# Order of a unit's high and low matmuls in the sequence stage of a fused FNet and GEGLU layer

## Chip, cores and metric

The kernel runs on one core of a Trainium2 chip. The metric is device time in microseconds of one execution of the whole program; lower is better. Times are medians of several runs.

## The reference

One token sequence of S = 2048 rows and D = 448 columns is normalised, goes through a Fourier mixing layer and through a gated feed-forward layer of width 1792, and the two results are multiplied and added to the input.

```python
xn = layernorm(x)                                   # (1, 2048, 448)
a = einsum("bsd,ed->bse", xn, dft_hid_re)
b = einsum("bsd,ed->bse", xn, dft_hid_im)
s = einsum("ts,bse->bte", dft_seq_re, a) - einsum("ts,bse->bte", dft_seq_im, b)
g = silu((gelu(xn @ w_gate) * (xn @ w_up)) @ w_down)
out = x + s * g
```

All inputs and the output are float32.

## The kernel before

**Numbers in two halves.** Matmuls read a float32 format that keeps fewer bits (`float32r`). To keep accuracy, an operand is split into a high half (the rounded value, made by ScalarE) and a low half (value minus high half, made by VectorE), and a product is summed from several matmuls: high by high, high by low, low by high.

**Stages.** Rows are in 16 blocks of 128. First come layer norm, transposes and the feed-forward layer with its Strassen-like schemes (`strassen`, `three`, `down_one`); then the transform along the hidden dimension (`hid_mm`, line 1105); then the last stage, the transform along the sequence, which this case is about. It starts at about 477 us of the span. The program is written in the order in which each engine issues it (`manual_schedule`), so the order of the calls in the code is the order on TensorE, ScalarE, VectorE, GpSimd and of the DMA queue of SyncE (SP).

**Last stage.** The output rows come in 8 groups, `j`, of two row blocks each. For each group the 16 blocks of input rows, `k`, are gone through. Fourteen of them (`KS`) are done with a scheme of Strassen's kind, in which the 2 by 2 product of (two output blocks) by (real and imaginary part) times (two halves of the columns) takes seven products. The other two (`KP`) are done plainly, as units `t0` and `t1`, line 1309 to 1311, 12 matmuls of 448 columns each. So a group has `UN` = 16 units, `m` counts the units of all groups, and `u` = `m % UN` is the place in the group; `NS` = 14.

A Strassen unit has 14 matmuls (`seven`). For each of the seven products `q` in the order of `PRODUCTS` (1, 6, 2, 7, 5, 3, 4) there is

- a *high* matmul (line 1289): high half of the coefficient block `i` as weights, 128 by 128, and the 448 columns `v` of the data tile `TS[k]`, block `b`, which holds high half and low half of 224 values beside each other;
- a *low* matmul (line 1292): low half of the same coefficient block, and the first 224 columns of `v` alone.

Each product has its own PSUM bank and is accumulated there over the fourteen units. The eighth bank takes `t0`; `t1` takes the bank that product 1 has left. For the next group the banks are rotated by one (`banks[1:] + banks[:1]`), so that its product 1 gets the bank in which product 6 was, and so on; the seventh gets that of `t0`.

**Around it.** The coefficient blocks of unit `m` are loaded from HBM by SP (`load_c`, lines 1181 to 1188), two of them are summed by VectorE (`sum_c`, lines 1194 and 1195), and `prep_c` splits them: ScalarE writes the high halves (line 149), VectorE the low ones (line 150), into one of four slots. In unit `m` the program issues, in this order: the matmuls; for `u` from 0 to 7, one DMA (line 1365) that overwrites a part of a data tile for the next group; `sum_c(m + 4)`; then what the unit's place asks for, in most `prep_c(m + 3)`, with `load_c(m + 8)` behind it.

**End of a group.** In the last Strassen unit (`u` = 13), `gather` combines the seven products: ScalarE copies product 1 from its bank (line 1317), and VectorE then goes through the others in the order 6, 2, 7, 5, 3, 4 (lines 1319 to 1325). Three of these operations are issued at `u` = 13, the rest behind `sum_c` at `u` = 14. The multiplication by the gate, the addition of the input and the stores follow in small steps during the next group.

**End of the kernel.** In the last group the last three Strassen units (`LAST` = 3) are not done one behind another. Their 21 steps (product, unit) are put in an order (`last_steps`) in which products 1, 6 and 2 are finished early and the others one by one:

```python
last_steps = [(q, n) for n, k in ((0, 4), (1, 3), (2, 3)) for q in order_[:k]]
last_steps += [(q, n) for q in order_[3:] for n in range(LAST) if (q, n) not in last_steps]
```

so steps 1 to 10 are products 1, 6, 2, 7 of the first unit, 1, 6, 2 of the second, 1, 6, 2 of the third. Step 8 finishes product 1. Behind them TensorE does `t0` and `t1`, while VectorE does `gather` and the final arithmetic (lines 1383 to 1402); the last stores are issued at line 1403.

Of the kernel before, what the change touches and what calls it, by code (L numbers as in the profile page):

```python
# [13 lines left out]
P = 128  # L14
S = 2048
D = 448
# [11 lines left out]
HD = D // 2  # L28
# [18 lines left out]
NS = len(KS)  # L47
# [4 lines left out]
def order(j):  # L52

    return [*KX[j % 2], *KR, *KX[(j + 1) % 2]]
# [5 lines left out]
def fnet_geglu(ctx: ExitStack, tc: tile.TileContext, xw, ca, ct, cp, et, wss, wd, out):  # L60
# [15 lines left out]
    nc = tc.nc  # L76
# [51 lines left out]
    def bank(i, name):  # L128
        return psum.tile([P, 512], F32, name=name, tag=f"b{i}")
# [421 lines left out]
    with tc.manual_schedule():  # L551
# [356 lines left out]
        h, l = [[v[:, n] for n in range(4)] for v in (xth[1], xtl[1])]  # L908
# [61 lines left out]
        for n, (p, f) in enumerate(blocks):  # L970
            g = f // 2
            dn, q = [send] * 4, tq[p]
# [8 lines left out]
            if p == 0:  # L981
# [12 lines left out]
                if f in (8, 11):  # L994

                    k = slice(0, 4, 3) if f == 8 else slice(1, 3)
                    for i in range(2):
                        v, w = [u[:, i * 2048 :][:, :2048] for u in (sp, a_x[1].bitcast(F32))]
                        v, w = [u.rearrange("p (k d) -> p k d", k=4)[:, k] for u in (v, w)]
                        nc.sync.dma_start(v, w)  # L1000
            elif f == 2:
                q = None
# [3 lines left out]
            elif f == 3:  # L1006

                late = then(late[0], t1_steps[7][2]), late[1]
                v = sb.tile([P, 8 * D], F32, name="gacc2", tag="u1")
# [3 lines left out]
                v = sb.tile([P, 4096], FR, name="w2", tag="u0")  # L1013
# [76 lines left out]
        TS, ab, behind = {}, {}, []  # L1090
# [4 lines left out]
        def hid_mm(k):  # L1095
            c, kk = divmod(k, 4)
            sl = slice(kk * P, (kk + 1) * P)
            ps = []
            for r in range(2):
                p = in_turn("x" if k < 2 else "all", f"ab{k}_{r}")  # L1100
                mm = [(xth[c][:, b, sl], e_at[b][r]) for b in range(4)]
                mm += [(xth[c][:, b, sl], e_at[b][2 + r]) for b in range(3)]
                mm += [(xtl[c][:, b, sl], e_at[b][r]) for b in range(4)]
                for n, (a, b) in enumerate(mm):
                    nc.tensor.matmul(p[:, :D], a, b, start=n == 0, stop=n == len(mm) - 1)  # L1105
                ps.append(p[:, :D])
            return ps
# [44 lines left out]
        units = [(j, k) for j in range(NK // 2) for k in order(j) + ["t0", "t1"]]  # L1152
        UN = NS + 2
# [43 lines left out]
        c_hl = {}  # L1197
# [15 lines left out]
        for k in [*range(14), 15, 14]:  # L1213
            ps = hid_mm(k)
# [54 lines left out]
                nc.sync.dma_start(gx[t], gv[:, 2 * j + t])  # L1269


        LOAD_AT = 2
        STORE_AT = 6, 9
        GX_AT, GX_END = (NS, 0), (11, 12)
# [2 lines left out]
        PRODUCTS = {1: (1, 0), 6: (3, 5), 2: (2, 2), 7: (5, 3), 5: (4, 4), 3: (6, 6), 4: (0, 1)}  # L1277
# [3 lines left out]

        def seven(m, ps, steps=None):

            for q, n in steps or [(q, 0) for q in PRODUCTS]:
                i, b = PRODUCTS[q]
                u = m + n
                v = TS[units[u][1]][:, b * D : (b + 1) * D]
                h, l = [w[:, i * P : (i + 1) * P] for w in c_hl[u]]
                nc.tensor.matmul(  # L1289
                    ps[q][:, :D], h, v, start=u % UN == 0, stop=False, skip_group_check=True  # L1290
                )
                nc.tensor.matmul(  # L1292
                    ps[q][:, :HD], l, v[:, :HD],
                    start=False, stop=u % UN == NS - 1, skip_group_check=True,
                )


        order_ = [*PRODUCTS]
# [45 lines left out]
        for m, (j, k) in enumerate(units):  # L1344
            u = m % UN
            end = j == NK // 2 - 1
            if u == 0:
                ps = {q: bank(banks[i], f"p{q}_{j}") for i, q in enumerate(PRODUCTS)}
            if k in KS:
                if not end or u < NS - LAST:  # L1350
                    seven(m, ps)
                elif u == NS - LAST:

                    seven(m, ps, last_steps)

                at = (0, 1, 2, 3, 4, 5, 6, 7) if j else range(LOAD_AT, LOAD_AT + 8)
                for i in range(8):
                    if u != at[i]:
                        continue
                    i, h = divmod(i, 4)  # L1360
                    TS[KX[(j + 1) % 2][i]] = TS[KX[j % 2][i]]
                    n = KX[(j + 1) % 2][i]
                    a, b = [v.rearrange("p (b d) -> p b d", d=D) for v in (TS[n], td[n])]
                    a, b = a[:, PARTS[h]], b[:, PARTS[h]]
                    nc.sync.dma_start(a.bitcast(F32), b)
            else:
                py = bank(banks[7 if k == "t0" else 0], f"py{k[1]}_{j}")
                plain(m, py)
# [131 lines left out]
```

## Time and profile before

| | us |
|---|---|
| median of 3 runs | 768.38 |
| lowest and highest | 768.17, 768.41 |
| profiled execution | 768.08 |
| its span in the profile | 766.3 |
| TensorE matmuls busy | 760.0 |
| weight loads busy (overlap with matmuls) | 685.6 |
| VectorE busy | 641.7 |
| ScalarE busy | 351.4 |

The profile is of one execution. PE is TensorE, PEld its weight loads, DVE is VectorE, ACT is ScalarE, POOL is GpSimd, SP is SyncE, whose queue issues most DMAs; SPq and ACTq are DMA issues of these engines. A row of the timeline has the start in us, the duration in us, the engine, the line of the kernel, the operation, the tiles that it writes and reads (out<-in), the shape, how many instructions are merged in the row, and in brackets how long the engine was idle before it and what ended this. A row of a group has busy us, mean ns of one, and idle time. Weight loads have a row of their own before the matmul that uses them. The recorded duration of a matmul is modelled and reaches beyond the start of the next one; the distance between two starts is the better measure of its cost. A matmul of float32r has a weight load of its own each time.

### The profile page before, as it was taken

How to read it: one execution, taken by the hardware profiler on the slowest of the kernel's cores; microseconds unless marked ns; L12 is line 12 of the kernel's file. 1: busy time of each engine (PE TensorE's matmuls, PEld its weight loads, DVE VectorE, ACT ScalarE, POOL GpSimd, SP SyncE). 2: the span in 40 equal slices, each digit the busy share in tenths (PEclk: the TensorE clock that was granted, in tenths of full speed). 3: DMA queues.
4: the chain of work that ended last, by engine and by line, in shares of the span. 5: the costliest groups of instructions: out<-in, count | busy, mean ns of one | idle time of the engine just before them, and what ended most of it. 6: DMA issues, size and time to landing. Idle time of an engine off the chain costs nothing.

```text
span 766.3 us, 11490 instructions
## 1 busy us (share of the span) xinstructions
PE 760.0 (99%) x4041; PEld 685.6 (89%) x4041; DVE 641.7 (84%) x1087; ACT 351.4 (46%) x499; POOL 122.8 (16%) x162
## 2 busy tenths in 40 slices
PE   9999999999999999999999999999999999999997
PEld 8988888888888888888889999999999999999997
DVE  7987789999989888988876677988889797979786
ACT  5866433444435334343344755544444344444441
POOL 2002332422434224232200000000000000000000
PEclk9999999999999999999999999999999999999999
DMA  8077484949568563738642732869696969788794
GB/s 299 15 223 233 118 246 138 233 154 243 205 142 298 139 207 82 223 79 245 153 184 85 296 165 69 279 224 338 209 352 206 341 213 311 248 279 277 246 324 153
DMA packets 81034, 162.28 MB, mean 212 GB/s; under 512 B 8016, under 2 KB 62800, under 8 KB 79568
## 3 DMA queue, kind: packets, MB, share of 16 engines
q1 hardware_dynamic: 75648, 135.02, 51.5%
q0 software_dynamic: 5184, 26.41, 16.1%
q8 instruction: 32, 0.52, 0.3%
q14 instruction: 26, 0.21, 0.1%
q10 hardware_dynamic: 144, 0.11, 0.0%
HBM read 139.36 MB, written 51.25 MB: 249 GB/s over the span
## 4 chain that ended last, share of the span: by engine, by line
PE 98%; DVE 1%; issue 0%; ACT 0%; DVEq 0%
PE x L444 24%; PE p L1289 21%; PE po L422 18%; PE p L1292 10%; PE ab L1105 9%; PE x L456 4%; PE gu L371 3%; PE gu L592 2%; PE py L1309 1%; PE py L1311 1%; PE py L1310 1%; PE pt L206 1%; PE warm L571 1%; PE pt L649 0%; DVE cc L1384 0%
## 5 line engine op out<-in xcount | busy, mean ns | idle before, releaser
L422 PE MATMUL po<-wd,hs 128*128 128x448 f32 x672 | 152.7, 366 | 0.0
L422 PEld LDWEIGHTS po<-wd,hs 128*128 128x128 f32 x672 | 125.8, 188 | 14.2
L444 PE MATMUL x<-xt,w 128*128 128x512 f32 x432 | 114.1, 391 | 0.0
L444 PEld LDWEIGHTS x<-xt,w 128*128 128x128 f32 x432 | 81.1, 188 | 15.3
L149 ACT ACTIVATE w<-raw 128x896 fp32r<-128x896 f32 (+1 forms) x59 | 53.6, 910 | 61.9 <-DVE raw L1195 22.4
L444 PE MATMUL x<-t,w 128*128 128x512 f32 x276 | 80.8, 391 | 0.0
L433 DVE TENSOR_TENSOR gacc<-gacc,po 128x448 f32<-128x448 f32 x96 | 58.5, 615 | 14.3 <-PE po L422 14.2
L1105 PE MATMUL ab<-w,xt 128*128 128x448 f32 x256 | 68.1, 365 | 0.0
L521 ACT ACTIVATE hs<-tmp 128x512 fp32r<-128x512 f32 x24 | 15.2, 633 | 101.1 <-DVE tmp L519 101.1
L444 PEld LDWEIGHTS x<-t,w 128*128 128x128 f32 x276 | 51.8, 188 | 9.3
L1289 PE MATMUL p<-xt,w 128*128 128x448 f32 x168 | 54.3, 374 | 0.0
L320 POOL TENSOR_TENSOR raw<-raw 128x256 f32<-128x256 f32 x23 | 19.7, 858 | 212.0 <-DMA raw<-wss 158.2
L1334 POOL DMA_DIRECT2D cc<-xw x14 | 12.3, 881 | 252.8 <-DVE raw L1194 96.1
L1105 PEld LDWEIGHTS ab<-w,xt 128*128 128x128 f32 x256 | 48.1, 188 | 3.8
L149 ACT ACTIVATE w<-f 128x896 fp32r<-128x896 f32 (+1 forms) x34 | 30.2, 888 | 41.7 <-DVE f L1195 17.4
L150 DVE TENSOR_TENSOR w<-raw,w 128x896 fp32r<-128x896 f32 (+1 forms) x40 | 41.8, 1046 | 2.0 <-ACT w L149 1.4
L339 ACT ACTIVATE w<-raw 128x768 fp32r<-128x768 f32 x24 | 20.3, 846 | 39.8 <-POOL raw L326 39.8
L1289 PE MATMUL p<-ts_g,w 128*128 128x448 f32 x112 | 36.3, 374 | 0.0
L1289 PE MATMUL p<-ts_u,ts_tmp 128*128 128x448 f32 x112 | 36.3, 374 | 0.0
L1289 PE MATMUL p<-hs,w 128*128 128x448 f32 x112 | 35.5, 374 | 0.0
L1105 PE MATMUL ab<-wd,xt 128*128 128x448 f32 x96 | 35.1, 365 | 0.0
L1289 PEld LDWEIGHTS p<-xt,w 128*128 128x128 f32 x168 | 31.5, 188 | 2.4
(297 smaller groups left out, 1849.6 us busy)
## 6 DMA issues: line engine op xcount, KB each, us to landing
sums<-ca SPq DMA_DIRECT2D x16, 896.0 KB, 8.8
sums<-ca POOLq DMA_DIRECT2D x16, 896.0 KB, 9.8
raw<-ct SPq DMA_DIRECT2D x69, 192.0 KB, 4.2
raw<-wss SPq DMA_DIRECT2D x24, 512.0 KB, 3.8
ts_u<-td SPq DMA_DIRECT2D x24, 448.0 KB, 5.7
ts_g<-td SPq DMA_DIRECT2D x24, 448.0 KB, 6.5
raw<-sums SPq DMA_DIRECT2D x69, 128.0 KB, 4.1
f<-ct SPq DMA_DIRECT2D x39, 192.0 KB, 4.5
```

Source lines behind the costliest of these rows:

```text
L149: nc.scalar.activation(h, src, AF.Copy)
L150: nc.vector.tensor_sub(l, src, h)
L320: eng.tensor_add(r[:, 1:16:14], r[:, 0:14:13], r[:, 9:17:7])
L339: nc.scalar.activation(h[:, :n], src[:, :n], AF.Copy)
L371: nc.tensor.matmul(ps[:, cols], a, xt[:, k, cols], start=n == 0, stop=n == len(mm) - 1)
L422: nc.tensor.matmul(po[:, :D], hs[:, a, kk * P : (kk + 1) * P], wdn[:, b, i], start=n == 0, stop=n == 5,)
L433: nc.vector.tensor_add(ga, ga, po[:, :D])
L444: nc.tensor.matmul(ps, a[i], b[j], start=first and n == 0, stop=n == 2, skip_group_check=True)
L456: nc.tensor.matmul(ps, a[0], x_, start=False, stop=True, skip_group_check=True)
L1105: nc.tensor.matmul(p[:, :D], a, b, start=n == 0, stop=n == len(mm) - 1)
L1289: nc.tensor.matmul(ps[q][:, :D], h, v, start=u % UN == 0, stop=False, skip_group_check=True)
L1292: nc.tensor.matmul(ps[q][:, :HD], l, v[:, :HD], start=False, stop=u % UN == NS - 1, skip_group_check=True,)
```

## The change

`seven` no longer issues high and low of each product in turn. It takes the steps in runs of `TOGETHER` = 7 and issues the high matmuls of a run first, then the low ones in the same order. A plain unit is one run; the 21 steps of the last three units are three runs: products 1, 6, 2, 7 of the first and 1, 6, 2 of the second unit; 1, 6, 2 of the third, 7 of the second and third, 5 of the first and second; and the rest of 5, 3 and 4. The flag that starts an accumulation stands on the high matmul of the group's first unit, the one that ends it on the low matmul of its last. Operands, counts, banks and everything on the other engines are as before.

```diff
+        TOGETHER = 7
...
         def seven(m, ps, steps=None):
 
-            for q, n in steps or [(q, 0) for q in PRODUCTS]:
-                i, b = PRODUCTS[q]
-                u = m + n
-                v = TS[units[u][1]][:, b * D : (b + 1) * D]
-                h, l = [w[:, i * P : (i + 1) * P] for w in c_hl[u]]
-                nc.tensor.matmul(
-                    ps[q][:, :D], h, v, start=u % UN == 0, stop=False, skip_group_check=True
-                )
-                nc.tensor.matmul(
-                    ps[q][:, :HD], l, v[:, :HD],
-                    start=False, stop=u % UN == NS - 1, skip_group_check=True,
-                )
+            steps = steps or [(q, 0) for q in PRODUCTS]
+            for at in range(0, len(steps), TOGETHER):
+                for part in range(2):
+                    for q, n in steps[at : at + TOGETHER]:
+                        i, b = PRODUCTS[q]
+                        u = m + n
+                        v = TS[units[u][1]][:, b * D : (b + 1) * D]
+                        w = c_hl[u][part][:, i * P : (i + 1) * P]
+                        d = D if part == 0 else HD
+                        nc.tensor.matmul(
+                            ps[q][:, :d], w, v[:, :d],
+                            start=part == 0 and u % UN == 0,
+                            stop=part == 1 and u % UN == NS - 1,
+                            skip_group_check=True,
+                        )
```

## The prediction

> **What bounds the kernel now.** I read the page first (busy times, then the chain that ended last), then single instructions of the last stage in the timeline.
>
> ```profile
> PE 760.0 (99%) x4041; PEld 685.6 (89%) x4041; DVE 641.7 (84%) x1087; ACT 351.4 (46%) x499; POOL 122.8 (16%) x162
> PE 98%; DVE 1%; issue 0%; ACT 0%; DVEq 0%
> L1289 PE MATMUL p<-xt,w 128*128 128x448 f32 x168 | 54.3, 374 | 0.0
> 546.00:580.00 34.00, 34.00 (x214) 32.36 (x213) 28.53 (x55) 15.47 (x18) 1.76 (x2) 1.00 0.89 287
> ```
>
> The page, the chain, a group of the high matmuls, and a stretch inside the last stage (columns: PE, PEld, DVE, ACT, POOL busy, granted clock, DMA share). TensorE carries 98% of the chain and has no idle time before the high matmuls; the clock is granted in full. VectorE, at 28.53 of 34 us, is behind it but not far. So the change is worth what it does to TensorE's pace, plus what it does where TensorE is not the last: the end.
>
> The pace first. These are the first high matmul of group 1, the first matmul behind its fourteen units, and from the chain a long run of matmuls of 448 columns, each with other weights than the one before.
>
> ```profile
> 512.65 0.36 PE L1289 MATMUL p<-ts_u,ts_tmp 128*128 128x448 f32 x1
> ...
> 543.35 0.38 PE L1309 MATMUL py<-ts_u,w 128*128 128x448 f32 x1
> 419.20 57.96 PE ab L1105 x286
> ```
>
> Fourteen units are 98 pairs of a high and a low: 30.70 / 98 = 0.3133 us a pair. A 448-column matmul behind another takes 57.96 / 286 = 0.2027 us. So a low (224 columns) costs 0.3133 - 0.2027 = **0.1106 us**, and everything turns on what it costs behind another low.
>
> **The change part by part.** No matmul, weight load, DMA or elementwise instruction is added or removed; only the order on TensorE differs, in 112 runs of seven products (8 groups of 14 units, the last three units of the last group being shared out over three such runs). In each run 7 lows stand in a row, so 6 x 112 = 672 lows are followed by a low instead of a high; six of seven highs are followed by a high. The trace of before has no low behind a low, and I bound it by neighbours.
>
> ```profile
> 561.28 0.19 PEld L1289 LDWEIGHTS p<-xt,w 128*128 128x128 f32 x1
> 561.38 0.38 PE L1289 MATMUL p<-xt,w 128*128 128x448 f32 x1
> 561.38 0.19 PEld L1292 LDWEIGHTS p<-xt,w 128*128 128x128 f32 x1
> 561.59 0.27 PE L1292 MATMUL p<-xt,w 128*128 128x224 f32 x1
> 561.59 0.19 PEld L1289 LDWEIGHTS p<-xt,w 128*128 128x128 f32 x1
> 561.69 0.37 PE L1289 MATMUL p<-xt,w 128*128 128x448 f32 x1
> 561.70 0.19 PEld L1292 LDWEIGHTS p<-xt,w 128*128 128x128 f32 x1
> ```
>
> Beside them, transposes and matmuls of 256 columns from the first stage (the same run of matmuls seen in two windows, one of which ends a matmul later).
>
> ```profile
> 45.78 0.60 PE L206 MATMUL pt<-ident,xr 128*128 128x128 f32 x4
> 46.11 0.30 PEld L422 LDWEIGHTS po<-wd,hs 128*128 128x128 f32 x2
> L206 PE MATMUL pt<-ident,xr 128*128 128x128 f32 x32 | 4.8, 272 | 0.0
> 13.78 0.88 PE L592 MATMUL gu<-xt,w 128*128 128x256 f32 x6
> 13.78 1.00 PE L592 MATMUL gu<-xt,w 128*128 128x256 f32 x7
> ```
>
> Each weight load starts when the matmul before its own starts, never earlier (561.28 beside the low before it, 561.38 with the high at 561.38, 561.59 with the low at 561.59): one load ahead and no more. Behind a low, the next load follows 0.10 to 0.11 us later (561.28 to 561.38, 561.59 to 561.70): the load of the next high's weights just fills the low's time. The transposes have only 128 columns to stream, and yet four of them, 0.272 us long each, span 0.60 us: (0.60 - 0.272) / 3 = 0.109 us apart, with the next load at 46.11 right behind the fourth's start. That is the pace of weight loads alone. Matmuls of 256 columns take 1.00 - 0.88 = 0.12 us each. A line through 448 and 256 columns (0.2027 and 0.120) puts the streaming of 224 columns at 0.106 us.
>
> So a low behind a low lies between 0.106 (streaming alone) and 0.120 (a matmul of 256 columns cannot be quicker than one of 224). I take the larger of loads and streaming, **0.109**: the 224-column low is nearest the transposes, which loads bound. It was bound by a load before, too, since a high's load ran under it; grouping does not change how many loads run under lows, seven per unit either way. That gains 672 x (0.1106 - 0.109) = **1.1 us**; at the bounds, 3.1 us gained or 6.3 us lost. The highs behind highs cost their 0.2027 in both orders. The first low of a unit, whose load waits for VectorE's low half, comes 1.42 us into the unit (7 x 0.2027) instead of 0.20, and the high half's wait on ScalarE keeps its place.
>
> Next, the ends of the groups. A product is complete with its low in the last unit. The first product, which ScalarE copies out and the whole combining in `gather` waits for, was complete 0.31 us into the unit and now is at 7 x 0.2027 + 0.11 = 1.53 us: **1.21 us later**. At the end of group 1:
>
> ```profile
> 541.16 0.37 PE L1289 MATMUL p<-ts_g,w 128*128 128x448 f32 x1
> 541.67 0.55 ACT L1317 ACTIVATE cc<-p 128x448 f32<-128x448 f32 x1 [1.93 <-PE p L1292]
> 542.24 0.62 DVE L1319 TENSOR_TENSOR cc<-cc,p 128x448 f32<-128x448 f32 x1 [0.81 <-ACT cc L1317]
> ...
> 547.16 0.62 DVE L1325 TENSOR_TENSOR cc<-p,cc 128x448 f32<-128x448 f32 x1
> ...
> 548.22 0.36 PE L1289 MATMUL p<-ts_u,ts_tmp 128*128 128x448 f32 x1
> ```
>
> ScalarE's copy moves from 541.67 to 542.9, and VectorE, which already waits for it (0.81 us idle), moves all its later work by 1.2 us: the last bank is read by 547.16 + 0.62 + 1.2 = 548.98. The next group starts at 548.22 and now takes all its banks within seven highs; the one just freed is the sixth's, at 548.22 + 5 x 0.2027 = 549.23. Spare: 0.25 us. Tight, but I cost it at nothing; if the spare were gone, every microsecond would be paid at seven group ends. Behind the late reads on VectorE stand the weight halves of the units ahead and, behind those, SP's loads of their raw blocks. The closest of these low halves that I found:
>
> ```profile
> 714.36 1.08 DVE L150 TENSOR_TENSOR xt<-raw,ts_tmp 128x896 fp32r<-128x896 f32 x1
> 716.83 0.38 PE L1289 MATMUL p<-ts_u,ts_tmp 128*128 128x448 f32 x1
> ```
>
> It is done at 715.44 and was wanted by the first low at 717.03; now that low comes at 716.83 + 1.42 = 718.25, so 1.2 us of delay leaves the old distance. SP's reloads of the tiles for the next group wait for a product of units 0 to 7 that finishes up to 1 us later, but have until unit 12. No cost.
>
> Last, the end of the kernel, where nothing covers that delay.
>
> ```profile
> 750.21 0.38 PE L1289 MATMUL p<-xt,w 128*128 128x448 f32 x1
> 752.61 0.27 PE L1292 MATMUL p<-ts_g,w 128*128 128x224 f32 x1
> 752.91 0.55 ACT L1317 ACTIVATE cc<-p 128x448 f32<-128x448 f32 x1 [0.80 <-PE p L1292]
> 753.50 0.62 DVE L1319 TENSOR_TENSOR cc<-cc,p 128x448 f32<-128x448 f32 x1 [0.66 <-ACT cc L1317]
> ...
> 755.48 0.62 DVE L1322 TENSOR_TENSOR cc<-cc,p 128x448 f32<-128x448 f32 x1
> ...
> 761.46 0.37 PE L1311 MATMUL py<-xt,ts_tmp 128*128 128x448 f32 x1
> 761.86 0.62 DVE L1400 TENSOR_TENSOR f<-ts_g,py 128x448 f32<-128x448 f32 x1
> 762.52 0.69 DVE L1402 TENSOR_TENSOR cc<-cc,f 128x224 f32<-128x224 f32 x2
> 753.50:763.20 9.70, 8.32 (x47) 7.47 (x45) 9.32 (x17) 0.00 (x0) 0.00 (x0) 1.00 0.13 42
> ```
>
> The last three units start at 750.21; the closing low of product 1, their eighth step, starts 2.40 us later at 752.61, ScalarE copies, and from 753.50 VectorE is busy 9.32 of 9.70 us to the end: a dense chain. L1400 starts just as the last matmul is done (761.46 + 0.37 = 761.83) and as VectorE itself is free. In the new order the steps go in three runs of seven, and step 8 is the first of the second run: its low stands behind one run (7 x 0.3133 = 2.19) and seven highs (1.42), 3.61 us in. The chain starts 3.61 - 2.40 = **1.2 us later**; the other products are complete before their turn (the fifth, product 5, closes with the first low of the third run, at 750.21 + 2 x 2.19 + 1.42 + 0.27 = 756.3, and is wanted at 755.48 + 1.2 = 756.7), so VectorE carries all of it to the last store.
>
> Sum, against the profiled execution's own 768.08 us (span 766.3 and 1.8 around it): 768.08 - 1.1 + 1.2 = 768.2. That execution lies 0.3 below the median of the three runs, 768.38, so on their scale **768.5 us**: no change, two small terms against each other.
>
> **The rivals.** *Lows in a row are dearer* (slower): a load may start only once the low before has really started, and streaming and loading may not overlap as fully as under a high. A line between 128 and 256 columns (0.109 and 0.120) gives 0.117 for 224: 672 x 0.008 = 5.4 us above my sum, 773.9. It decides early: with 1.2 us lost at the end, 0.111 a low is already over 0.2%. For it: both limits lie within 3 ns of each other, and nothing in the trace shows them together. Against: 256 columns hide a load at 0.120 with nothing visible on top.
>
> *Group ends run dry* (slower): if VectorE's reads come 0.5 us later than I count, TensorE waits 0.25 us seven times, 1.8 us: 770.3. For: the spare is small. Against: the reads move rigidly with ScalarE's copy.
>
> *Loads get ahead* (faster): if the lows' weights were loaded while highs stream, a low would take the 0.101 us that stands between its start and the next high's. 672 x 0.0096 = 6.5 us, with the end's loss 763.1 on the runs' scale. The rows above, one load ahead each time, speak against it. The Trainium skill speaks for it, page "TensorE: Matmul & The Clock Gate", section "Back-to-back issue gap": loads are pulled ahead through a 64-deep window and 128-column matmuls are sustained at about 81 ns, 512-column ones at 131. By a line through these, an estimate from that page, a low would take 93 ns and the sum be about 757; the trace's 0.11 us for 128 columns and 0.2027 for 448 disagree with both figures, so I go by the trace.
>
> That the change does not do what it says I leave out: the order on TensorE is the order of the program.
>
> **How the numbers follow.** No change, 0.48, with its own range of 767.4 to 769.9 (0.107 to 0.111 a low). Lows dearer, 0.27; group ends or a wait I have not seen, 0.10; loads ahead or another gain, 0.15. A measurement of this kernel tells about 0.2% (1.5 us) from no change: faster 0.15, same 0.48, slower 0.37. The range takes in part of the dearer lows and a gain of two microseconds: 766.2 to 772.6, with about a tenth left out on each side.
>
> **What would show it.** Right: a timeline with lows 0.109 apart and highs 0.203, a unit of 2.18 us instead of 2.19, the copy L1317 1.2 us later in the last unit of each group, and VectorE's last instruction about 1.2 us further behind the last matmul. Wrong: lows at 0.111 or more, or under 0.106; idle time on TensorE at the first highs of a group; weight loads starting more than one matmul ahead.

## The result, and the profile after

| | before | after |
|---|---|---|
| median of 7 runs, us | 768.33 | 770.69 |
| lowest and highest, us | 768.00, 768.41 | 770.57, 770.92 |
| span of the profiled execution, us | 766.3 | 768.9 |

The changed kernel takes 2.36 us more, a ratio of 1.0031 (95% interval 1.0022 to 1.0040). That is above the 0.2% at which I drew the line: it is slower. In the two profiled executions the last stage, from its first matmul to the end of the span, takes 291.72 us instead of 289.30, 2.42 us more, so the whole difference arises there (the other 0.2 us of the two spans lie ahead of it, where nothing was changed). It has three parts: the start of the stage, the pace, and the end.

**The start.** The timeline of the changed kernel at the first unit of the stage (start, duration, engine, line, tiles, and in brackets the idle time and what ended it):

```profile
477.21 2.12 PE L1295 MATMUL p<-ts_u,ts_tmp 128*128 128x448 f32 x7
477.80 0.61 DVE L1113 SCALAR_TENSOR_TENSOR xt<-ab,xt 128x448 fp32r<-128x448 f32 x1
478.29 0.53 ACT L1123 ACTIVATE f<-ab 128x448 f32<-128x448 f32 x1
478.46 0.19 PEld L1295 LDWEIGHTS p<-ts_u,ts_tmp 128*128 128x128 f32 x1 [0.34 <-DVE xt L1113]
478.86 0.19 PEld L1295 LDWEIGHTS p<-ts_u,ts_tmp 128*128 128x128 f32 x1 [0.21 <-ACT f L1123]
...
479.95 0.38 PE L1295 MATMUL p<-ts_g,w 128*128 128x448 f32 x1
```

The first high of the stage and that of the second unit, before:

```profile
477.00 0.36 PE L1289 MATMUL p<-ts_u,ts_tmp 128*128 128x448 f32 x1
...
479.19 0.38 PE L1289 MATMUL p<-ts_g,w 128*128 128x448 f32 x1
```

The first seven highs, which should span 7 x 0.2027 plus the tail of the last one, about 1.58 us, take 2.12. The sixth waits until VectorE has read a bank in which the stage before had left its sums (L1113, done at 478.41), the seventh until ScalarE has (L1123, done at 478.82). The whole unit takes 2.74 us by its unrounded starts, against 2.19 before. The second unit no longer waits for its low half and is 0.05 us shorter. Together **0.5 us**. My prediction looked at the ends of the eight groups and not at the start of the first.

**The group ends** did hold. After group 1:

```profile
542.02 2.36 PE L1295 MATMUL p<-ts_g,w 128*128 128x448 f32 x14
543.75 0.55 ACT L1322 ACTIVATE cc<-p 128x448 f32<-128x448 f32 x1 [2.24 <-PE p L1295]
544.33 0.62 DVE L1324 TENSOR_TENSOR cc<-cc,p 128x448 f32<-128x448 f32 x1 [0.86 <-ACT cc L1322]
549.24 0.62 DVE L1330 TENSOR_TENSOR cc<-p,cc 128x448 f32<-128x448 f32 x1
549.10 1.58 PE L1295 MATMUL p<-ts_u,ts_tmp 128*128 128x448 f32 x7
```

ScalarE's copy starts 1.73 us into the unit instead of 0.51, the 1.2 us that were forecast, and VectorE reads the last bank until 549.86. The next group's seven highs from 549.10 still take the 1.58 us of an undisturbed row.

**The pace.** First high of group 1 and first matmul behind its fourteen units, then one row of lows, the same row from its third low on, and the high behind it:

```profile
513.43 1.58 PE L1295 MATMUL p<-ts_u,ts_tmp 128*128 128x448 f32 x7
544.22 0.37 PE L1314 MATMUL py<-ts_u,w 128*128 128x448 f32 x1
...
550.31 0.95 PEld L1295 LDWEIGHTS p<-ts_u,xt 128*128 128x128 f32 x7
550.52 0.94 PE L1295 MATMUL p<-ts_u,xt 128*128 128x224 f32 x7
550.73 0.72 PE L1295 MATMUL p<-ts_u,xt 128*128 128x224 f32 x5
550.85 0.41 PEld L1295 LDWEIGHTS p<-ts_u,xt 128*128 128x128 f32 x3
551.29 0.58 PE L1295 MATMUL p<-ts_g,w 128*128 128x448 f32 x2
```

A unit takes 30.79 / 14 = 2.199 us (2.200 by the unrounded starts) instead of 30.70 / 14 = 2.193. Seven highs at 0.2027 leave 2.199 - 1.419 = 0.780 for seven lows: 0.1115 each, where by turns it was 0.1106 and I had forecast 0.109. (By turns only the pair can be measured, 0.3133 us; the 0.1106 takes its high at the 0.2027 of the other highs.) The five lows from 550.73, 0.27 us long each, span 0.72: (0.72 - 0.27) / 4 = 0.11 apart; the three loads from 550.85, 0.19 long each, are (0.41 - 0.19) / 2 = 0.11 apart. Over 112 units **0.7 us** more, not 1.1 us less.

**The end.**

```profile
755.54 0.55 ACT L1322 ACTIVATE cc<-p 128x448 f32<-128x448 f32 x1 [0.84 <-PE p L1295]
756.11 0.62 DVE L1324 TENSOR_TENSOR cc<-cc,p 128x448 f32<-128x448 f32 x1 [0.69 <-ACT cc L1322]
762.88 0.37 PE L1316 MATMUL py<-xt,ts_tmp 128*128 128x448 f32 x1
764.47 0.61 DVE L1405 TENSOR_TENSOR f<-ts_g,py 128x448 f32<-128x448 f32 x1
765.12 0.69 DVE L1407 TENSOR_TENSOR cc<-cc,f 128x224 f32<-128x224 f32 x2
756.10:764.40 8.30, 7.14 (x39) 6.34 (x37) 7.94 (x14) 0.00 (x0) 0.00 (x0) 1.00 0.12 31
```

L1405, which was L1400 before, needs the last matmul, done at 763.25, but comes at 764.47, because VectorE's chain, dense again (7.94 of 8.30 us), began with product 1 and that closed late. From the start of the last matmul to the end of the span it is 6.05 us instead of 4.84: **1.2 us**. The three parts, 0.5 + 0.7 + 1.2 = 2.4, make up the whole.

### The profile page after: what moved, and what is told of

It reads as the page before. It is cut to its first block, busy times and chain, and to the rows that moved or that the text cites. A ratio compares the mean times of both kernels' runs of the same rounds, so it can differ in the third digit from the quotient of the medians.

```text
span 768.9 us, 11490 instructions
## 1 busy us (share of the span) xinstructions
PE 761.9 (99%) x4041; PEld 686.3 (89%) x4041; DVE 640.5 (83%) x1087; ACT 351.2 (46%) x499; POOL 124.5 (16%) x162
## 4 chain that ended last, share of the span: by engine, by line
PE 95%; DVE 2%; issue 1%; ACT 1%; DVEq 0%; ACTq 0%
PE p L1295 32%; PE x L444 24%; PE po L422 18%; PE ab L1105 6%; PE x L456 4%; PE gu L371 3%; PE gu L592 2%; PE py L1314 1%; PE py L1315 1%; PE py L1316 1%; PE pt L206 1%; PE warm L571 1%; ACT hs L1141 0%; DVE xt L1144 0%; ACT xt L1141 0%
## 5 line engine op out<-in xcount | busy, mean ns | idle before, releaser
L433 DVE TENSOR_TENSOR gacc<-gacc,po 128x448 f32<-128x448 f32 x96 | 58.5, 615 | 16.2 <-PE po L422 15.9
L521 ACT ACTIVATE hs<-tmp 128x512 fp32r<-128x512 f32 x24 | 15.2, 633 | 99.7 <-DVE tmp L519 99.7
L1295 PE MATMUL p<-xt,w 128*128 128x448 f32 (+1 forms) x224 | 44.8, 343 | 0.0
L1295 PEld LDWEIGHTS p<-xt,w 128*128 128x128 f32 x224 | 37.3, 189 | 2.0
L1295 PE MATMUL p<-ts_g,w 128*128 128x448 f32 (+1 forms) x224 | 39.0, 320 | 0.0
L1295 PEld LDWEIGHTS p<-ts_g,w 128*128 128x128 f32 x224 | 35.2, 190 | 1.7
L1295 PE MATMUL p<-hs,w 128*128 128x448 f32 (+1 forms) x224 | 36.5, 320 | 0.0
L1295 PEld LDWEIGHTS p<-hs,w 128*128 128x128 f32 x224 | 34.2, 190 | 1.7
```

Of the source, the lines that this page charges most:

```text
L433: nc.vector.tensor_add(ga, ga, po[:, :D])
L1295: nc.tensor.matmul(ps[q][:, :d], w, v[:, :d], start=part == 0 and u % UN == 0, stop=part == 1 and u % UN == NS - 1, skip_group_check=True,)
```

## Experiments

"The last stage" in the table is the time from its first matmul to the end of the span, "a unit" the distance from the first high of group 1 to the first matmul behind its fourteen units, divided by fourteen, "the end" the distance from the start of the last matmul to the end of the span; all from the starts in each trace. The last stage starts at 477.0 to 477.6 us in these traces, though no edit touches what lies ahead; that is why it is timed from its first matmul. The kernel before, measured beside them, had medians of 768.32 (first to fourth), 768.38 (fifth to eighth) and 768.36 us.

| kernel | median us | first unit | a unit | the end | last stage |
|---|---|---|---|---|---|
| before | 768.33 | 2.185 | 2.193 | 4.84 | 289.30 |
| after | 770.69 | 2.736 | 2.200 | 6.05 | 291.72 |
| e1, end by turns | 770.16 | 2.749 | 2.199 | 5.10 | 290.74 |
| e2, first unit by turns | 770.30 | 2.185 | 2.200 | 6.05 | 291.16 |
| e3, both by turns | 769.77 | 2.185 | 2.199 | 5.34 | 290.38 |
| e4, only the end grouped | 769.62 | 2.185 | 2.193 | 6.03 | 290.49 |
| e5, lows of 192 columns, grouped | 770.64 | 2.731 | 2.199 | 6.02 | 291.70 |
| e6, lows of 192 columns, by turns | 769.12 | 2.166 | 2.192 | 4.85 | 290.04 |
| e7, lows of 128 columns, grouped | 771.92 | 2.706 | 2.206 | 5.98 | 292.78 |
| e8, lows of 256 columns, grouped | 776.81 | 2.812 | 2.253 | 5.94 | 297.60 |
| e9, all ends and first unit by turns | 769.14 | 2.185 | 2.201 | 4.86 | 290.05 |
| e10, lows with the highs' weights | 771.07 | 2.745 | 2.199 | 6.25 | 291.86 |

### Where the time goes

The first four undo one part, or do one part alone. All have this edit of the changed kernel, each with one of the four conditions:

```diff
+            together = 1 if steps else TOGETHER                          # e1
+            together = 1 if m == 0 else TOGETHER                         # e2
+            together = 1 if steps or m == 0 else TOGETHER                # e3
+            together = TOGETHER if steps else 1                          # e4
             steps = steps or [(q, 0) for q in PRODUCTS]
-            for at in range(0, len(steps), TOGETHER):
+            for at in range(0, len(steps), together):
                 for part in range(2):
-                    for q, n in steps[at : at + TOGETHER]:
+                    for q, n in steps[at : at + together]:
```

> The changed kernel, but the 21 steps of the last three units have high and low by turns again. Theory: of the 2.4 us that the change cost, 1.2 us come from product 1 closing later at the end, so this takes 769.5 us, and from the last matmul to the end of the span pass 4.85 us instead of 6.05. Rival: the end only shows a delay that the pace and the start of the stage have made; then the end stays about 6 us and the time at 770.7.

> The changed kernel, but the very first unit of the stage has high and low by turns again. Theory: the first seven highs wait for banks that the stage before still holds, 0.5 us in all, so this takes 770.2 us, and the first unit 2.19 us instead of 2.74. Rival: the wait moves into the second unit, which then takes over 2.4 us, and the time stays at 770.7.

> First unit and last three units by turns, the other 108 units grouped. Theory: what is left over the kernel before is the pace alone, 8 ns a unit or 0.8 to 0.9 us: 769.1 us. Rival (the lows in a row gain, as I predicted, and the loss lies elsewhere): 767.3 us.

> The kernel before, but the last three units grouped in runs of seven. Theory: 1.2 us above the kernel before, 769.5 us, with 6.05 us from the last matmul to the end of the span. Rival (the end is paid only together with the rest): 768.3 us.

e4 bears out the end in full: alone it costs 1.2 us of the stage and 1.3 us of the median. e2 bears out the start: the first unit is back at 2.185 us, the stage is 0.55 us shorter, the median 0.4 us lower, and the wait does not reappear in the second unit (2.20 us).

e1 and e3 missed: both ended half a microsecond or more above what I expected. The pace is as forecast; what is off is the end, 5.10 and 5.34 us where 4.85 was expected, though the steps of the last three units stood as before. The traces show 0.25 and 0.5 us of the miss there. The executions that were profiled took 769.79 and 769.34 us, about 0.4 us less than the medians; what the slower ones lose beyond this is in no trace. The timeline of e1 shows what took over:

```profile
753.96 0.63 ACT L149 ACTIVATE ts_tmp<-raw 128x512 fp32r<-128x512 f32 x1 [1.08 <-DMA raw<-cp]
754.50 0.53 ACT L1323 ACTIVATE cc<-p 128x448 f32<-128x448 f32 x1
754.62 0.69 DVE L150 TENSOR_TENSOR ts_tmp<-raw,ts_tmp 128x512 fp32r<-128x512 f32 x1 [0.70 <-ACT ts_tmp L149]
755.23 0.61 DVE L1325 TENSOR_TENSOR cc<-cc,p 128x448 f32<-128x448 f32 x1
```

The copy of product 1 (L1323) is here not idle for the product; it queues on ScalarE behind the high half of the last plain unit, and that waits for its coefficients from HBM. VectorE goes straight from that unit's low half to the combining, without a gap. Here that high half starts 8.9 us before the last matmul (at 762.90); in the kernel before it was 10.0 us (751.48 and 761.46), and ScalarE then waited 0.80 us for the product:

```profile
751.48 0.63 ACT L149 ACTIVATE ts_tmp<-raw 128x512 fp32r<-128x512 f32 x1 [0.49 <-DMA raw<-cp]
```

So something makes the preparation late towards the end. The changed group ends were the suspect: each lets VectorE start 1.2 us later on `gather`, and the low halves and, behind them, SP's loads, are late by as much. e9 tests it:

```diff
+            together = 1 if steps or m == 0 or m % UN == NS - 1 else TOGETHER
```

> First unit, last Strassen unit of every group and the last three units by turns, the other 101 units grouped. With the first unit and the last three units by turns alone, 5.34 us still passed from the last matmul to the end of the span, with VectorE's and SP's work about 1.5 us late before it. Theory: that lateness comes from the group ends, where product 1 closes 1.2 us later; with them by turns the end takes 4.85 us again and what is left is 101 x 8 ns = 0.8 us of pace: 769.1 us, and the last stage from its first matmul to the end of the span 0.8 us longer than before. Rival: the lateness comes from the grouped units themselves (later release of what they read); then the end stays at 5.3 us and the time at 769.7 us.

It came as the theory said: 769.14 us, the end at 4.86, the stage 0.75 us longer than before. The same two engines in e9:

```profile
752.92 0.63 ACT L149 ACTIVATE ts_tmp<-raw 128x512 fp32r<-128x512 f32 x1 [1.07 <-DMA raw<-cp]
753.58 0.69 DVE L150 TENSOR_TENSOR ts_tmp<-raw,ts_tmp 128x512 fp32r<-128x512 f32 x1 [0.68 <-ACT ts_tmp L149]
754.19 0.55 ACT L1323 ACTIVATE cc<-p 128x448 f32<-128x448 f32 x1 [0.64 <-PE p L1296]
754.77 0.62 DVE L1325 TENSOR_TENSOR cc<-cc,p 128x448 f32<-128x448 f32 x1 [0.50 <-ACT cc L1323]
```

ScalarE waits for the product again. The traces also show the way in between. These are VectorE's first low half behind the last `gather` ahead of the last group, and SP's issue of the coefficients of the last plain unit, each in the kernel before, in e1 and in e9:

```profile
725.56 1.08 DVE L150 TENSOR_TENSOR w<-raw,w 128x896 fp32r<-128x896 f32 x1
728.16 1.08 DVE L150 TENSOR_TENSOR w<-raw,w 128x896 fp32r<-128x896 f32 x1
726.75 1.08 DVE L150 TENSOR_TENSOR w<-raw,w 128x896 fp32r<-128x896 f32 x1
745.26 0.44 SPq L1185 DMA_DIRECT2D raw<-cp  x1
747.74 0.38 SPq L1185 DMA_DIRECT2D raw<-cp  x1
746.71 0.40 SPq L1185 DMA_DIRECT2D raw<-cp  x1
```

The low half starts 35.9, 34.7 and 36.0 us before the last matmul (761.46, 762.90 and 762.73), the issue 16.2, 15.2 and 16.0 us. So in e1 both are late, by 1.2 and 1.0 us, and in e9 they are back within 0.2 us of their old places. The low half just ahead of that `gather` is not late in e1 (43.0 us before the last matmul, against 42.6), so this one group end makes the lateness; that of the earlier ones, if any, has been made up by then.

So product 1's late close delays the end twice over: directly in the last three units, and, behind that and hidden by it, through the group end before them. Undoing the first alone gives back 1.0 us of the stage in the traces and 0.5 of the median (e1), and uncovers the second; with both undone (e9) the end is as before.

### What paces a low

The rest, 0.7 us of pace, is small, but it is the term that I had with the wrong sign. Is a low behind a low held by its stream, by the load of the next weights, or by the two so close together? Four widths of the low product, grouped (e5, e7, e8) and by turns (e6):

```diff
-                        d = D if part == 0 else HD
+                        d = D if part == 0 else 192        # e5; e7: 128; e8: 256
```

```diff
-        TOGETHER = 7
+        TOGETHER = 1
...
-                        d = D if part == 0 else HD
+                        d = D if part == 0 else 192        # e6
```

> The changed kernel with lows of 192 columns instead of 224 (the last 32 columns of each low product are left out). If loads alone pace the lows, a unit stays at 2.200 us. If streaming alone does, each low loses 32 columns, 13 ns, and a unit takes 2.107 us (10 us less in all). If the 112 ns are a near tie of the two, a low falls to the 109 ns of the transposes and stops there: a unit of 2.18 us, 2 us less in all.

> High and low by turns with lows of 192 columns (the last 32 columns of each low product are left out). If a low by turns is held by the load of the next high's weights, a unit stays at 2.192 us and the time at 768.3 us. If it streams, a unit takes 2.099 us, 10 us less in all.

> The changed kernel with lows of 128 columns (96 columns of each low product are left out). Loads alone: a unit stays at 2.200 us. Near tie: 2.18 us, as with 192 columns. Streaming alone: 40 ns less a low, a unit of 1.92 us.

> The changed kernel with lows of 256 columns (32 columns too many, so the products are other ones). All theories let streaming win here: 120 ns a low as in the first stage, a unit of 2.26 us, 6 us more in all. A low much above 120 ns would show a cost of the seven banks or of the order itself, and not of load and stream.

Group 1 of e5 and of e7, first high and first matmul behind its units:

```profile
513.36 0.77 PE L1295 MATMUL p<-ts_u,ts_tmp 128*128 128x448 f32 x3
544.14 0.39 PE L1314 MATMUL py<-ts_u,w 128*128 128x448 f32 x1
```

```profile
513.56 0.97 PE L1295 MATMUL p<-ts_u,ts_tmp 128*128 128x448 f32 x4
544.45 0.42 PE L1314 MATMUL py<-ts_u,w 128*128 128x448 f32 x1
```

30.78 / 14 = 2.199 us a unit with 192 columns and 30.89 / 14 = 2.206 with 128: nothing is gained by narrower lows, not even with 96 columns fewer. The 7 ns more of e7 are not in its lows. Its second and third unit of group 1, from first high to first high:

```profile
515.71 2.39 PE L1295 MATMUL p<-ts_g,w 128*128 128x448 f32 x14
517.93 2.36 PE L1295 MATMUL p<-ts_tmp,w 128*128 128x448 f32 x14
520.13 0.42 PE L1295 MATMUL p<-xt,w 128*128 128x448 f32 x1
```

One takes 2.22 us, the next 2.20, and so on in turn. By the unrounded starts the highs are 0.206 us apart in the longer units and 0.203 in the others, while a low costs 0.1116 us on average, as in the other grouped runs with up to 224 columns. By turns (e6) a unit with 192 columns takes 2.192, as with 224. With 256 columns a low takes 119 to 120 ns, as in the first stage, and the stage 5.9 us more than with 224, near the forecast. So up to 224 columns **the loads alone pace the lows, in both orders**; neither streaming nor a near tie plays a part. A load costs 0.1106 us behind one low by turns and 0.1115 in a row of lows, not the 0.109 of the transposes. One thing I do not explain: matmuls of 448 columns come at two paces, not only in e7. The units of e6 are as forecast, but two of its plain matmuls, eleven apart, show

```profile
544.35 0.37 PE L1316 MATMUL py<-ts_u,w 128*128 128x448 f32 x1
546.62 0.37 PE L1315 MATMUL py<-ts_u,w 128*128 128x448 f32 x1
```

2.27 / 11 = 0.206 us; over all of them it is 0.207 us from one to the next, instead of 0.203, which by itself makes up the 0.7 us by which its median lies above the kernel before.

> The changed kernel, but the low matmuls load the high half of the coefficient block as weights (the product of the low halves is left out and the high one added twice in part). If the 112 ns of a low behind a low come from where its weights lie, or from a wait for the low half, they change, to 109 ns as for the transposes if that is the pace of any load; if it is the load of such weights behind a short matmul as such, a unit stays at 2.200 us.

```diff
-                        w = c_hl[u][part][:, i * P : (i + 1) * P]
+                        w = c_hl[u][0][:, i * P : (i + 1) * P]
```

A unit stays at 2.199 us. So it is neither that the low weights lie elsewhere than the high ones nor a wait for VectorE's half. The end of this kernel is 0.2 us longer than that of the changed one (6.25 us), which I do not explain.

## Why the forecast came out as it did, point by point

I called no change the likeliest, at 768.5 us, with 0.37 for slower. The time, 770.69, lies inside the range and 0.8 us above the likeliest case's own; slower by 0.31% is what happened. That it lies in the range is due to the range's width: the sum itself is 2.2 us too low, about 1.8 of it by the pace and 0.5 by the start of the stage. (Two small figures beside the sum do not come out of it either: 0.107 us a low gives 767.2 us and not 767.4, and 0.111 a low with the end's 1.2 gives 1.5 us, at the 0.2% and not over it.)

- *The end, +1.2 us.* Right in place, cause and size: 6.05 against 4.84 us, and 1.2 us with the end alone (e4). What I did not see is that the same delay, through the last group end before it, lay a second time behind it (e1, e3, e9).
- *A low behind a low, "I take the larger of loads and streaming, 0.109", -1.1 us.* This is the step that failed. That the loads bound it was right, and so was "grouping does not change how many loads run under lows". But then the price was already in the trace of before: the low by turns, held by a load, at 0.1106. I took the 0.109 of the transposes as the load's own pace instead and made a gain of 1.6 ns, 672 times, out of the difference of two rows of different kinds. It measures 0.1115: 0.7 us lost. That the lows come out dearer than by turns at all, by 0.9 ns each, stays without a cause.
- *The start of the stage.* Not in the sum at all, 0.5 us. I checked seven group ends for banks that are taken sooner, found 0.25 us to spare, and left out the eighth place where seven banks are taken for the first time, from another stage.
- *Group ends run dry.* A rival that did not come: no wait at the seven ends, in spite of 0.25 us.
- *Lows in a row are dearer.* The rival that won in kind, by the point I gave, "0.111 a low is already over 0.2%": it was 0.1115. Its price, 0.117 from a line between 128 and 256 columns, lies seven times as far above 0.1106 as what was measured (6.4 against 0.9 ns), for the cost is flat up to 224 columns (e5, e7) and rises only where streaming takes over (e8).
- *Loads get ahead.* It did not happen: a row of lows has its loads 0.11 us apart. The Trainium skill's section "LDWEIGHTS (loading the stationary operand)", on the page "TensorE: Matmul & The Clock Gate", has a load's time go by the number of weight columns; its formula gives 107 ns for 128, an estimate. The runs have loads of 128 columns alone, at 0.109 to 0.112 us, so they are near the figure and cannot show the rule. The 81 ns that its section "Back-to-back issue gap" states for 128-column matmuls is not seen here even with lows of 128 columns.

## What to carry to other kernels

In this kernel, where every matmul brings new weights, a matmul of 192 or 224 columns cost the 0.110 to 0.112 us of a weight load in either order, and so did one of 128 columns in a row of its kind. Reordering did not help, for the same number of loads ran under narrow matmuls. The price to use is that of the same kind of matmul in the same stage, not of a cleaner neighbour. An order that puts off the first result of an accumulation is paid where that result starts a long chain on another engine, above all at the end of the kernel. When an order takes buffers sooner, check every place where they change hands, the first one too.

## Not expected of the hardware

A load of 128 weight columns behind a short matmul took 0.1115 us in a row of lows with 224 columns and the same with 192 and 128, while the transposes of the first stage had their loads 0.109 apart. Why these loads are 2 to 3 ns dearer stays open; that the low halves lie elsewhere than the high ones is ruled out (e10). The two paces of 448-column matmuls, 0.203 and 0.206 to 0.207 us at a granted clock of 0.999 and 0.998 (e6, e7), stay open too.
